# Seven products instead of eight in the second matmul of an MLP: Strassen's scheme on two token tiles of an RWKV-6 + MLP kernel

## Chip, cores and metric

One core of one Trainium2 chip. The metric is the device time of one execution in microseconds (us); 11 runs of the kernel before are known, and one profiled execution. Engines: PE (matmuls; PEld its weight loads), DVE, ACT and POOL (elementwise), SP (issues DMAs). Each works through its own instructions in order and waits on semaphores for the others.

## What is computed

All arrays are float32; B = 4, H = 8 heads, S = 768 steps, D = 48 (so 384 = H·D per token).

```python
state = 0
for t in range(S):                        # RWKV-6, per batch and head
    cur = einsum('bhd,bhe->bhde', u*k[t], v[t])
    y[t] = einsum('bhd,bhde->bhe', r[t], state + cur)
    state = w[t][..., None]*state + einsum('bhd,bhe->bhde', k[t], v[t])
x = y as (B, S, 384)
xn = (x - mean) / sqrt(var + 1e-6) * g_ln
out = x + relu(xn @ w_ch1) @ w_ch2        # w_ch1: 384 x 1536, w_ch2: 1536 x 384
```

## The kernel before, in words

**Work units.** A round is one batch and half of the sequence: 384 tokens, in three tiles of 128. There are eight rounds (0 to 7). A round has two units of four heads each; unit q belongs to round q // 2.

**Recurrence.** For a unit, r and k lie turned, channels on partitions and time along the free axis (`rkT`), and the decays w likewise. Six levels (0 to 5) build the in-chunk attention matrix: at each level `quads` (96 small PE matmuls into `a_ps` for the two units of a round) computes blocks, `grow` (DVE, one 128x768 op for each unit) multiplies r and k by decays for the next level, and `keep` (DVE, a predicated copy) moves the blocks out of PSUM. So quads of a level need the grow of the level before. After level 5 come `ends` (four PE transposes of k into `kn_ps`, each copied by ACT), then `states` (PE `kv`, then a chain of small DVE ops), and `own_outputs`/`outputs` (PE `y`, added up by DVE into `x`).

**Own term.** u·k·r is made from r and k in natural layout (`nat`): `own_products` on DVE in turn 2 and on POOL later, `own_sums` on DVE, `own_term` on POOL. `nat["k"]` and `nat["r"]` have two buffers, by unit parity.

**Loading.** SP issues nearly all DMAs in one queue: `load` (natural layout, three DMAs a tensor), `load_before`, `stage` (runs of w, k, r in four `raw` buffers, shared in turn), the stores. `squares` (DVE 32x32 transposes) turns a staged run into `wT` or `rkT` and so frees its buffer. Rounds 1 and 2 use PE transposes instead.

**MLP.** `moments`/`norm` (DVE, ACT) give `xn`, `turned_x` (PE transposes, ACT) gives `xT`. `mlp` is a generator. It yields after each of 12 steps of the first product (three 128x128x384 matmuls into `h_ps`; ACT's relu writes `h`) and after each of 12 steps of the second (three matmuls into `o_ps`, twelve for a token tile; a DVE add of x, a store). A step is six passes on PE, as a float32 matmul is two passes in the profile. The PSUM tiles `h_ps` and `o_ps` come from one pool, `ps_m`, with two buffers taken in turn; the transposes' PSUM (`ps_t`) also has two.

**Order.** `InOrder` keeps PE, ACT, DVE and POOL (and what goes through `SPO`) in the order in which the program is written; what is issued through `SP` may be placed by the scheduler. The loop `for rnd in range(1, NR + 1)` (called turn 1 to 8 here) does the recurrence of round rnd, level by level, and beside it fills PE with steps of earlier rounds' MLPs. In each of 48 slots (turn, level), `fill(UNTIL[slot], tasks)` spreads the slot's tasks evenly among as many MLP steps as bring the count to `UNTIL`. From slot 17 on, `UNTIL` grows by `MLP_STEPS // NLEV`, 24 // 6 = 4. The MLP of round rnd - 1 joins the list after level 4 of turn rnd (after level 2 in turn 2). The first product so falls into levels 5 to 1, the second into levels 1 to 4 of the next turn. What is left after turn 8, the MLP of round 7, runs by itself.

In the trace of before, turn 2 runs from about 105 to 158 us, turn 3 to 215, and turns 4, 5, 6 and 7 start near 215, 278, 340 and 403 us. Turn 8 starts near 466 us, and the last MLP at 510.7.

## Time and profile before

| | |
|---|---|
| median of 11 runs | 562.02 us (559.16 to 564.7) |
| profiled execution, own time | 562.52 us |
| its span, first to last instruction | 560.8 us |
| mean granted TensorE clock | 0.990 |
| PE busy | 546.8 us (97%) |
| DVE busy | 332.5 us (59%) |
| PE matmuls `h_ps`, 128x384 | 576 passes, 197.2 us |
| PE matmuls `o_ps`, 128x384 | 576 passes, 197.4 us |
| PE small matmuls `a_ps` | 4128, 71.0 us |
| PE's share of the chain that ended last | 81% (DVE 9%, SP queue 4%) |

The profile puts nearly every instruction at line 49 (the helper that records it), so instructions are told apart by the tiles they write and read: `o_ps<-w_sb,h` is the second product, `rkT<-rkT,tot` a grow, `A<-mask,a_ps` a keep, `own_ps<-sel,ruk` an early sum with a moving operand of two columns. A row of a timeline has the start in us, the length, the engine, the operation, out<-in with shapes, and in brackets the idle time ahead of it and what ended it.

### The profile page before, as it was taken

How to read it: one execution, taken by the hardware profiler on the slowest of the kernel's cores; microseconds unless marked ns; L12 is line 12 of the kernel's file. 1: busy time of each engine (PE TensorE's matmuls, PEld its weight loads, DVE VectorE, ACT ScalarE, POOL GpSimd, SP SyncE). 2: the span in 40 equal slices, each digit the busy share in tenths (PEclk: the TensorE clock that was granted, in tenths of full speed). 3: DMA queues.
4: the chain of work that ended last, by engine and by line, in shares of the span. 5: the costliest groups of instructions: out<-in, count | busy, mean ns of one | idle time of the engine just before them, and what ended most of it. 6: DMA issues, size and time to landing. Idle time of an engine off the chain costs nothing.

```text
span 560.8 us, 18190 instructions
## 1 busy us (share of the span) xinstructions
PE 546.8 (97%) x7898; PEld 358.7 (64%) x7898; DVE 332.5 (59%) x654; ACT 169.1 (30%) x363; POOL 135.8 (24%) x157
## 2 busy tenths in 40 slices
PE   9999999998899999999999999999999999999997
PEld 6786665665556666666666666666666666665554
DVE  4889998869688775666585746666563612030000
ACT  3567887502160026201521025201530025202200
POOL 6131010303384029201670039021740000000000
PEclk9889999999989999999999999999999999999999
DMA  9947787155566465646464636444200000000000
GB/s 232 219 104 146 182 222 187 44 115 103 153 150 135 141 130 132 132 114 121 114 125 117 150 94 141 111 128 101 58 1 15 18 15 1 2 29 15 0 15 28
DMA packets 141552, 56.64 MB, mean 101 GB/s; under 512 B 124448, under 2 KB 130720, under 8 KB 141472
## 3 DMA queue, kind: packets, MB, share of 16 engines
q1 hardware_dynamic: 139600, 54.88, 41.7%
q8 instruction: 62, 1.02, 0.7%
q10 hardware_dynamic: 1872, 0.59, 0.4%
q14 instruction: 18, 0.15, 0.1%
HBM read 48.66 MB, written 4.72 MB: 95 GB/s over the span
## 4 chain that ended last, share of the span: by engine, by line
PE 81%; DVE 9%; SPq 4%; ACT 2%; DMA 2%; issue 1%; DVEq 0%; ACTq 0%
PE o_ps L49 32%; PE h_ps L49 27%; PE a_ps L49 9%; PE y L49 4%; DVE w_sb L49 3%; DVE rkT L49 3%; SPq L163 2%; PE kv L49 2%; PE idle L49 2%; PE kn_ps L49 2%; PE xT_ps L49 1%; PE w_ps L49 1%; PE own_ps L49 1%; PE k_ps L49 1%; PE r_ps L49 1%
## 5 line engine op out<-in xcount | busy, mean ns | idle before, releaser
L49 PE MATMUL h_ps<-xT,w_sb 128*128 128x384 f32 x576 | 197.2, 492 | 2.8 <-DVE o L49 1.4
L49 PE MATMUL o_ps<-w_sb,h 128*128 128x384 f32 x576 | 197.4, 492 | 0.1
L49 PEld LDWEIGHTS h_ps<-xT,w_sb 128*128 128x128 f32 x576 | 106.1, 191 | 70.7 <-DVE o L49 2.0
L49 PEld LDWEIGHTS o_ps<-w_sb,h 128*128 128x128 f32 x576 | 105.4, 190 | 65.2 <-ACT h L49 1.0
L49 DVE TENSOR_TENSOR rkT<-rkT,tot 128x768 f32<-128x768 f32 (+1 forms) x96 | 78.5, 859 | 28.6 <-issue 16.9
L49 ACT ACTIVATE h<-h_ps 128x384 f32<-128x384 f32 x96 | 46.9, 489 | 143.9 <-PE h_ps L49 143.7
L49 PEld LDWEIGHTS a_ps<-rkT 48*64 48x64 f32 x4128 | 66.0, 137 | 21.9 <-issue 9.8
L49 PE MATMUL a_ps<-rkT 48*64 48x32 f32 x4128 | 71.0, 221 | 1.2 <-DVE rkT L49 1.0
L49 DVE TENSOR_TENSOR o<-o_ps,x 128x384 f32<-128x384 f32 x24 | 13.3, 553 | 95.9 <-PE o_ps L49 95.9
L49 POOL TENSOR_TENSOR vo<-v,own 128x576 f32<-128x576 f32 x16 | 19.5, 1219 | 96.3 <-DVE own L49 54.8
L49 ACT ACTIVATE rstd<-mv,eps 128x3 f32<-128x3 f32 x8 | 2.4, 296 | 130.1 <-DVE mv L49 130.1
L49 DVE SCALAR_TENSOR_TENSOR s<-s,decay,kv 128x48 f32<-128x48 f32 x160 | 29.3, 258 | 18.6 <-PE kv L49 18.6
L49 POOL TENSOR_TENSOR nat_w<-nat_w,nat_r 128x576 f32<-128x576 f32 x10 | 15.1, 1506 | 104.2 <-DMA nat_w<-in_v_dram 68.6
L49 DVE COPY_PREDICATED A<-mask,a_ps 128x768 f32<-128x768 int8 x32 | 38.4, 1200 | 0.0
L49 DVE TENSOR_TENSOR x<-y,vo 128x288 f32<-128x288 f32 x32 | 13.1, 451 | 30.9 <-PE y L49 30.1
L49 ACT ACTIVATE xT<-xT_ps,g_sb 128x384 f32<-128x384 f32 x24 | 13.6, 580 | 48.4 <-PE xT_ps L49 48.4
L49 DVE TENSOR_TENSOR rkT<-rkT,wT 128x768 f32<-128x768 f32 x16 | 24.9, 1592 | 0.9 <-PE a_ps L49 0.8
L49 DVE TENSOR_REDUCE own<-rk 128x12 f32<-128x576 f32 x12 | 8.9, 740 | 22.5 <-POOL rk L49 22.4
L49 DVE TENSOR_SCALAR w_sb<-w_sb 128x384 f32<-128x384 f32 (+1 forms) x48 | 19.5, 407 | 0.8
L49 PE MATMUL kn_ps<-ident,rkT 128*128 128x128 f32 x96 | 14.4, 285 | 4.0 <-DVE rkT L49 3.1
L49 DVE STREAM_TRANSPOSE rkT<-r_runs 128x384 f32<-128x384 f32 x20 | 15.6, 836 | 4.4 <-DMA r_runs<-in_r_dram 4.4
L49 PEld LDWEIGHTS y<-v,A 64*64 64x64 f32 x384 | 12.8, 134 | 7.6 <-issue 4.9
(88 smaller groups left out, 543.8 us busy)
## 6 DMA issues: line engine op xcount, KB each, us to landing
raw<-in_moe_w_ch_dram SPq DMA_DIRECT2D x24, 384.0 KB, 3.9
w_runs<-in_w_dram SPq DMA_DIRECT2D x79, 70.0 KB, 2.0
k_runs<-in_k_dram SPq DMA_DIRECT2D x79, 70.0 KB, 1.9
r_runs<-in_r_dram SPq DMA_DIRECT2D x79, 70.0 KB, 1.9
v<-in_v_dram SPq DMA_DIRECT2D x48, 96.0 KB, 2.8
out_dram<-o SPq DMA_DIRECT2D x24, 192.0 KB, 2.2
nat_r<-in_r_dram SPq DMA_DIRECT2D x42, 96.0 KB, 3.4
nat_k<-in_k_dram SPq DMA_DIRECT2D x42, 96.0 KB, 3.2
```

Source lines behind the costliest of these rows:

```text
L49: return lambda *args, **kw: self.tc.keep_in_program_order(f(*args, **kw))
L163: eng.dma_start(out=t[ds(HP * j + SQ * e, SQ), 0:n], in_=bass.AP(tensor=src.tensor, offset=first + SQ * e, ap=[[NS * D, SQ], [1, n]]),)
```

## The change

**Second product.** For rounds 2 to 7, `seven` takes the place of the twelve steps. Token tile 2 (Z) stays a plain product, in four steps of three 384-column matmuls. Token tiles 0 and 1 with the halves of the inner dimension (even and odd blocks f, called e) and of the output columns (n) form 2x2 blocks, and seven products of six 128x128x192 matmuls each take the place of eight. They go into the PSUM tiles X and Y (from `ps_m`, with Z the third) and V (from `ps_t`). Steps in order: Z, Z, X, V, V, Z, Z, X (with S2), Y, X (with S3), Y: 11 instead of 12.

**Sums.** DVE makes four sums of 128x768 of the hidden activations for each round (S3, the even block of which V's first product is made, S2, and a last one in place for Y), and adds the products to x in place: seven adds of 192 columns and two of 384, instead of three of 384. `passed()` writes queued sums and adds behind the product of the step in which they come up; the adds of Z, X and Y follow one another near the end, and `y_ps` takes the PSUM buffer of `z_ps`.

**Weight sums.** `weight_sums` computes differences of blocks of `w_ch2` once, on DVE, in slots 17, 18 and 19 (turn 3 level 5, turn 4 levels 0 and 1); one of them in place in `w2_sb`. Their room is a new tile `more` and the second buffers of `nat["k"]` and `nat["r"]`. Units from 8 on therefore use the first buffers alone, and the second unit's k and r are loaded later in the turn (level 4), after POOL is done with the first unit's.

**Turn 2.** r-u-k products and sums: the first unit's at level 2 as before, the second unit's at level 3; its load of k and r for the next round moves with it. DVE transposes of unit 6's r go from level 4 to level 5, where those of unit 7's k and r are too.

**Memory and count.** `hs` is one tile in place of twelve, `low` is a tile in place of a pool, `xn` lies in `kn` buffers (round 0: in a used `rkT`), and `o` is gone. `MLP_STEPS` is 23, and `UNTIL` grows by 23/6.

On DVE the built program has, in turns 4 to 6, this order between the quads of levels 3 and 5: grow, grow, keep (level 3); statistics and norm; three transposes; two adds of V; a transpose; the in-place sum over hs; grow, grow, keep (level 4); the adds of Z, X, Y, X, Y. PE's order there: quads of level 3, V's second step, Z's last two steps, quads of level 4, two groups of `xT` transposes, X with S2, a third group, Y, X with S3, Y, quads of level 5.

```diff
+    def natural(nm, q):
+        return nat[nm][q % 2 if q < 4 * U else 0]
...
-        groups = ((0, 1), (2,)) if rnd == 0 else ((0,), (1,), (2,))
...
-                o = p2.tile([P, H, D], F32, tag="o", name=f"o{name}_{i}")
-                DVE.tensor_tensor(out=o, in0=ps[i], in1=x[:, i], op=ALU.add)
...
+        if rnd > 1:
+            yield from seven(rnd, x, store)
+            return
...
+    def weight_sums(c):
+        if c == 1:
+            DVE.tensor_tensor(out=B_[:, 0, 1], in0=B_[:, 0, 1], in1=B_[:, 0, 0], op=ALU.subtract)
+            return
+        for at, t in pieces(c):
+            n = ds(at, t.shape[1])
+            DVE.tensor_tensor(
+                out=t, in0=more[:, n] if c == 4 else B_[:, 1, 1, n],
+                in1=B_[:, 1, 0, n] if c == 4 else B_[:, 0, 1, n], op=ALU.subtract,
+            )
...
+        Z = tile_of("z_ps")
+        both = [lambda m, e=e: w2_sb[:, 2 * m + e, :] for e in range(2)]
+        product(Z, A(2, 0), both[0], True, range(M // 2))
+        yield
+        sums(S3, A_[:, 0, 0], A_[:, 0, 1], ALU.subtract)
+        product(Z, A(2, 0), both[0], False, range(M // 2, M))
+        yield
+        add(2, 1, Z[:, 0:HD])
+        sums(A_[:, 0, 1], A_[:, 0, 1], A_[:, 1, 1], ALU.add)
+        X = tile_of("x_ps")[:, 0:HD]
+        product(X, A(0, 0), B(0, 0), True)
+        yield
+        add(0, 0, X)
+        sums(S2, A_[:, 0, 1], A_[:, 0, 0], ALU.subtract)
+        V = ps_t.tile([P, RN], F32, tag="t", name=f"v_ps{rnd}")
+        product(V[:, 0:HD], A(0, 1), B(1, 0), True)
+        yield
+        product(V[:, HD:], A(1, 1), lambda m: T(4, m), False)
+        yield
+        add(0, 0, V[:, 0:HD])
+        add(1, 0, V[:, HD:], ALU.subtract)
+        product(Z, A(2, 1), both[1], False, range(M // 2))
+        yield
+        sums(A_[:, 1, 0], A_[:, 1, 0], S2, ALU.subtract)
+        product(Z, A(2, 1), both[1], False, range(M // 2, M))
+        yield
+        due.append(lambda: DVE.tensor_tensor(out=x[:, 2], in0=Z, in1=x[:, 2], op=ALU.add))
+        due.append(lambda: store(2))
+        product(X, lambda m: S2[:, m], lambda m: T(2, m), False)
+        add(0, 1, X)
+        passed()
+        yield
+        Y = tile_of("y_ps")[:, 0:HD]
+        product(Y, A(1, 0), B(0, 1), True)
+        add(1, 1, Y)
+        passed()
+        yield
+        product(X, lambda m: S3[:, m], lambda m: T(3, m), False)
+        yield
+        add(1, None, X)
+        product(Y, A(0, 1), B(1, 1), False)
+        add(0, 1, Y)
+        passed()
+        store(0)
+        store(1)
+        yield
+
+    MLP_STEPS = FC + TT * (FC // KC) - 1
...
-        UNTIL.append(UNTIL[-1] + MLP_STEPS // NLEV)
+        UNTIL.append(UNTIL[-1] + MLP_STEPS / NLEV)
...
-            if rnd == 2 and lev == 2:
-                for q in now:
-                    tasks += each(own_products, [q], [DVE]) + each(own_sums, [q])
-                    tasks += each(load, new[q % U :][:1], "kr")
+            if rnd == 2 and lev in (2, 3):
+                tasks += each(own_products, now[lev - 2 :][:1], [DVE])
+                tasks += each(own_sums, now[lev - 2 :][:1])
+                tasks += each(load, new[lev - 2 :][:1], "kr")
...
+            if slot in (17, 18, 19):
+                tasks += each(weight_sums, ((3,), (1,), (2, 4))[slot - 17])
...
-                if m >= 0:
-                    tasks += each(squares, *turns[m], pairs)
-                if m < 2:
-                    tasks += each(stage, *turns[m + 1], pairs)
+                if rnd == 2 and m > 0:
+                    tasks += each(squares, new[:1], "kr"[m - 1], pairs)
+                    tasks += each(stage, new[1:], "kr"[m - 1], pairs)
+                    if m == 2:
+                        tasks += each(squares, new[1:], "kr", pairs)
+                else:
+                    if m >= 0:
+                        tasks += each(squares, *turns[m], pairs)
+                    if m < 2:
+                        tasks += each(stage, *turns[m + 1], pairs)
...
             if rnd > 1 and new and lev == chain:
                 tasks += each(own_products, new[:1], [POOL])
+                if rnd > 2:
+                    tasks += each(load, new[1:], ["kr"])
```

## Prediction

> **What bounds it now.** I read the page first (busy shares, slices), then PE's waits, then timelines of single engines.

> ```profile
> PE 546.8 (97%) x7898; PEld 358.7 (64%) x7898; DVE 332.5 (59%) x654; ACT 169.1 (30%) x363; POOL 135.8 (24%) x157
> ```
> ```profile
> PE kn_ps L49 <- DVE rkT L49: 3.1, 2, 2.7
> PE h_ps L49 <- DVE o L49: 1.4, 1, 1.4
> ```
> PE is the bound. Its waits are few, and the two largest lie in turn 2 of the loop (at 153.4 and 135.4 us); from 171 us on it never waits over 0.5 us. So a matmul taken away gives back its time unless a new wait eats it. The price of one is in PE's timeline of the last stage and of an early one:
> ```profile
> 533.91 23.38 PE L49 MATMUL o_ps<-w_sb,h 128*128 128x384 f32 x72
> ```
> ```profile
> 20.31 1.50 PE L49 MATMUL own_ps<-sel,ruk 128*128 128x2 f32 x12 [0.24 <-ACT wT L49]
> ```
> A logical product is two passes. 72 passes start within 23.38 us less the last one's 0.16 of pipeline: 322.5 ns each. The own_ps passes stream only 2 columns and still follow at some 112 ns (1.50 less 0.27 over 11): that is the pace of loading 128x128 weights.

> DVE matters too, because Strassen's sums go to it. Its timeline in turn 5 from the level-3 quads on, then PE's in the same stretch:
> ```profile
> 312.11 1.83 DVE L49 TENSOR_TENSOR rkT<-rkT,tot 128x768 f32<-128x768 f32 x2 [2.22 <-issue]
> 313.85 0.96 DVE L49 COPY_PREDICATED A<-mask,a_ps 128x768 f32<-128x768 int8 x1
> 314.72 1.47 DVE L49 BATCH_NORM_STATS2 stats<-x 128x6 f32<-128x384 f32 x3
> ...
> 318.16 1.53 DVE L49 STREAM_TRANSPOSE rkT<-k_runs 128x384 f32<-128x384 f32 x2
> 319.55 1.52 DVE L49 STREAM_TRANSPOSE rkT<-r_runs 128x384 f32<-128x384 f32 x2
> 320.92 0.53 DVE L49 TENSOR_TENSOR o<-o_ps,x 128x384 f32<-128x384 f32 x1
> 321.38 1.80 DVE L49 TENSOR_TENSOR rkT<-rkT,tot 128x768 f32<-128x768 f32 x2
> 323.10 1.00 DVE L49 COPY_PREDICATED A<-mask,a_ps 128x768 f32<-128x768 int8 x1
> ```
> ```profile
> 312.62 6.07 PE L49 MATMUL o_ps<-w_sb,h 128*128 128x384 f32 x18
> 318.62 1.60 PE L49 MATMUL a_ps<-rkT 48*64 48x32 f32 x96
> 320.15 0.55 PE L49 MATMUL xT_ps<-ident,xn 128*128 128x128 f32 x3
> 320.53 2.10 PE L49 MATMUL o_ps<-w_sb,h 128*128 128x384 f32 x6
> ```
> DVE works here without a break from 312.1 to 324.1. Nothing on PE needs its end before the quads at 329.0, so it has 5 us to spare. The change spends them.

> **PE work removed.** Of each MLP from round 2 on (six), 48 passes of 384 columns become 84 of 192. A pass of 192 is in no row: by proportion 161.3 ns; the recorded length of a weight load, 190, is the upper end. I take 162.5, by the 384 row it is nearest to: the load's pace of 112 lies below it. 48 x 322.5 = 15.48 us; 84 x 162.5 = 13.65; six times 1.83 = **-10.98**. At 190 ns it would be 504 x 27.5 ns = 13.9 us worse. [...] The sum goes by the row: whatever is fixed in a pass is part of its 322.5.

> **New wait at Y (levels 4 of turns 4 to 6).** Y takes Z's PSUM buffer (two in `ps_m`), so its first pass waits for the add `x[:, 2] += Z`. In DVE's program order that add stands behind grow and keep of level 4. DVE from the first grow of level 3, start to start in turn 5: grow 2 x 0.87, keep 0.87, statistics and norm 3.44, three transposes 2.08, two adds of V 0.56 (192 columns, from the 0.37 of 288 and 0.46 of 384), transpose 0.69, the sum over hs 0.87 (768 elements, as a grow), grow 2 x 0.86, keep 0.9, the Z add 0.55: 13.42. 312.11 + 13.42 = 325.53. PE: V's second half 1.95 and Z's second half 3.87 take the place of the 18 passes, quads end as before at 320.15, two groups of xT 0.71, X 1.95, the third xT 0.35: ready at 323.2. It waits 2.35 us (0.4 of it at the second xT, which needs V's PSUM buffer back). Turns 4 and 6 show the same rows within 0.3. 3 x 2.35 = **+7.05**. Behind Y stand X, Y's second product, the level-5 quads and all the rest of PE; nothing gives it back, since DVE then waits for PE. Turn 7 has no transposes (2.8 us less): **+0.35**. Turn 8 and the last MLP have no grows: 0. Bounds for one wait: 1.3 (if sums and adds share more of their start) to 3.5 (POOL doubled a keep to 1.88 us elsewhere).

> **Fewer steps, other order.** 23 steps in place of 24 leave seven h steps, not eight, between the level-5 quads and the level-1 quads. DVE's grow of level 0 ends 18.9 us after the level-5 quads, hanging on POOL; PE needs it at 19.6, so it still holds (0.7 to spare). But kn transposes now come three in a row, and the third needs the first one's PSUM copied (ACT 0.47, behind the relu): 0.45 at four turn ends, **+1.8** (0 to 2).

> **Weight sums, turn 4.** 4,608 elements at 959 ns for 768 are 5.8 us of DVE, once. The first 1.4 lie in DVE's wait for POOL (5.6 us idle after 209.0); the next 1.4 stand behind grow of level 0, where all but 0.4 is idle time; the last 2.9 stand in front of the w transposes, which so start 3.3 us later, at 232.9 where it was 229.6. The k and r runs take over their buffers: SP issues them in 8.2 us from the first free buffer (16 at about 0.47, with one long one), the last ends near 242.0 and lands 1.9 later (the median of the issues' view), where DVE wants it at 241.5, since PE arrives 1.5 us earlier. Behind that transpose in DVE's queue are S3, the first Z add and the sum that V's first product needs: 243.9 + 0.7 + 0.9 + 0.3 + 0.9 = 246.7. PE would be there at 244.9. Without the long issue 0.9 is left of these 1.8; I take **+1.4** (0 to 2.5).

> **Turn 2.** Here DVE and SP are late:
> ```profile
> 148.56 0.86 DVE L49 STREAM_TRANSPOSE rkT<-r_runs 128x384 f32<-128x384 f32 x1 [2.27 <-DMA r_runs<-in_r_dram]
> 150.25 0.85 DVE L49 STREAM_TRANSPOSE rkT<-r_runs 128x384 f32<-128x384 f32 x1 [0.83 <-DMA r_runs<-in_r_dram]
> ```
> Unit 5's r-u-k products (2.36 us) go behind the last o add, which ends the 1.4 us wait of h_ps; unit 6's r transposes go behind grow of level 5, which ends the 2.7. PE then runs some 6 us ahead, up to the level-1 quads of turn 3. Those need grow of level 0, and before it in DVE's queue stands unit 7's r transpose. SP now issues six nat loads after unit 5's product (135.6 to 138.8) and six more before r_runs7 (0.55 us each), so this run's last issue ends near 158.0 (156.1 before), landing 1.9 later. Transpose, sums, states and two grows after it: 168.0, where before it was 170.0: -2.0. PE then stands over 3 us, and the rows show what follows such a wait (last columns: PEclk, DMA share, GB/s):
> ```profile
> 150.70:153.40 2.70, 0.01 (x1) 0.00 (x0) 2.66 (x6) 0.49 (x1) 1.50 (x2) 1.00 0.56 159
> 153.40:157.40 4.00, 3.61 (x12) 2.46 (x13) 4.00 (x3) 1.43 (x3) 3.92 (x3) 0.57 0.54 149
> ```
> A low clock after the wait: the matmuls lost about 0.8 us by it. In before that was paid here, after the change it is paid a turn later, perhaps for longer; I charge 0.4 net: **-1.6** (-4 to +1).

> **End.** The last add is 192 wide (-0.2), a second store is issued behind the first (0.33): **+0.15**. Edits at nothing: hs, low and xn in other memory (same order of use), outputs added in place, k and r of one unit loaded later. In turn 5 that load waits on SP for POOL's last use (325.0); behind it in the queue stand two stores and `load_before`, whose own releases come later still. It lands near 330 and POOL takes it at 336.8 at the earliest; were that cover gone, up to 3.4 us a turn.

> **Sum.** -10.98 + 7.05 + 0.35 + 1.8 + 1.4 - 1.6 + 0.15 = -1.8. The profiled execution took 562.52 us (span 560.8, with 1.7 around it), 0.5 above the median of the 11 runs, 562.02: it would take 560.7, the median **560.2**. Its own range, from the bounds that don't move together: 557 to 563.5.

> **Rivals.** (a) The cover at Y holds, because DVE gets through its queue 2.4 us sooner than these rows add up: no 7.4 us of waits, 552.8. For it: DVE is only 59% busy. Against: the stretch above has no gap to give. (b) Slower: the Y waits trip the clock. At Y 1.95 us pass in one piece; 1.4 did not drop the clock at 135.4, 2.7 did at 153.4. A drop costs half of 3.4 us, three times 1.7 = 5.1: 565.3. It decides from a wait of somewhere between those two. [...] (c) Loads do not hide under 192 columns and a pass takes 190 ns: 574.1. Against: the 112 of own_ps.

> **Chances.** Forecast 0.62 (0.36 below -0.3%, 0.21 within, 0.05 above; 0.3% or 1.7 us is about what can be measured here), (a) 0.18, (b) 0.15 (0.03 within, 0.12 slower), (c) 0.05. Faster 0.54, same 0.24, slower 0.22. The range 552.5 to 565.5 leaves out (c), half of (a) and the end of (b).

> **What would show it.** Right: 192-column passes 160 to 165 ns apart; PE idle about 2 us before `y_ps` in turns 4, 5, 6, ended by DVE, and hardly in 7; turns 4 to 6 no shorter than the 62.6 us of before, turn 8 and the last MLP each 1.8 shorter; waits at 135 and 153 gone, one of 2 to 5 us at the first quads of turn 3. Wrong: no wait at `y_ps`, half clock after it, or passes at 190.

## The result and the profile after

The changed kernel takes 570.24 us (median of 12 runs, 567.37 to 572.88); the kernel before, run beside it, 563.09 (47 runs). The ratio is 1.0134, 95% interval 1.0113 to 1.0155: slower by some 7.5 us, where 560.2 was forecast. The profiled execution took 567.69 us (span 566.0), so the median holds about 2.5 us more than the trace shows.

The busy shares and the shares of the chain that ended last, from the page of after:

```profile
PE 541.4 (96%) x8114; PEld 388.4 (69%) x8114; DVE 372.1 (66%) x720; ACT 169.8 (30%) x363; POOL 140.1 (25%) x157
```
```profile
PE 59%; DVE 21%; DMA 5%; SPq 5%; ACT 4%; issue 4%; POOL 1%; DVEq 0%; ACTq 0%; POOLq 0%
```

PE is busy 5.4 us less than before, and yet the span is 5.2 us longer. DVE's share of the last chain went from 9% to 21%: PE now waits for it. Its waits by tile say where:

```profile
PE a_ps L49 <- DVE rkT L49: 5.5, 3, 4.6
PE y_ps L49 <- DVE x L49: 4.5, 4, 2.1
PE kn_ps L49 <- ACT kn L49: 2.7, 8, 0.6
PE xT_ps L49 <- DVE x L49: 2.2, 2, 2.0
```

Columns: total us, times, longest. In before, kn_ps (3.1) and h_ps (1.4) stood at the top, both in turn 2. That of h_ps is gone and that of kn_ps is down to 0.5. In their place one wait of 4.6 stands before quads, and y_ps, xT_ps and the third kn group wait once a turn. (In the text below a wait is counted from start to start of passes less the nominal pass, so it is 0.1 to 0.2 longer than in these lists.)

**Turn by turn.** Turn 2 is entered 0.45 us ahead of before, and turn 3's first outputs end 2.9 us behind it. Turns 4, 5 and 6 take 65.9, 64.0 and 64.3 us where they took 62.6; turn 7 takes 62.1 for 63.1.

**Turn 2, in DVE's and SP's queues.** DVE's timeline of after, then the SP queue's:

```profile
153.74 1.54 DVE L49 STREAM_TRANSPOSE rkT<-r_runs 128x384 f32<-128x384 f32 x2
155.13 1.51 DVE L49 STREAM_TRANSPOSE rkT<-k_runs 128x384 f32<-128x384 f32 x2
159.15 0.86 DVE L49 STREAM_TRANSPOSE rkT<-r_runs 128x384 f32<-128x384 f32 x1 [2.50 <-DMA r_runs<-in_r_dram]
161.51 0.87 DVE L49 STREAM_TRANSPOSE rkT<-r_runs 128x384 f32<-128x384 f32 x1 [1.50 <-DMA r_runs<-in_r_dram]
...
166.08 3.76 DVE L49 TENSOR_TENSOR rkT<-rkT,wT 128x768 f32<-128x768 f32 x2
```
```profile
151.74 1.49 SPq L176 DMA_DIRECT2D nat_w<-in_k_dram  x3
153.33 2.21 SPq L176 DMA_DIRECT2D nat_w<-in_v_dram  x3
155.64 3.70 SPq L165 DMA_DIRECT2D r_runs<-in_r_dram  x8
```

The r runs of unit 7 are issued from 155.64 to 159.34. Two things end just ahead of that: the loads of `nat_w` (155.54), and unit 6's r transposes (155.28), which free the staging buffers. Unit 7's last r transpose ends at 162.4, and the chain behind it (sums, states, grow of level 0) at 169.85. The kernel before came to the same grow at 169.97. So DVE gained nothing, while PE, freed of its two waits, came to the quads 5 us earlier and stood. The same place on PE, and the stage by windows (us, busy us of PE, PEld, DVE, ACT, POOL with counts, then PEclk, DMA share, GB/s):

```profile
167.85 1.51 PE L49 MATMUL a_ps<-rkT 48*64 48x32 f32 x48 [4.57 <-DVE rkT L49]
169.90 1.51 PE L49 MATMUL a_ps<-rkT 48*64 48x32 f32 x48 [0.54 <-DVE rkT L49]
```
```profile
162.54:165.95 3.41, 0.75 (x48) 0.62 (x44) 3.38 (x15) 0.04 (x1) 2.76 (x3) 1.00 0.55 155
...
167.85:171.31 3.46, 2.92 (x96) 2.75 (x96) 3.35 (x8) 0.00 (x0) 3.23 (x4) 0.50 0.67 129
171.31:176.19 4.88, 4.88 (x12) 2.73 (x9) 4.88 (x12) 0.86 (x2) 3.36 (x5) 0.50 0.20 38
```

PEclk is 0.50 from 165.95 to 176.19, 10.24 us. The second quads take 1.51 us, 0.6 longer than at full clock, and the o passes behind them follow at 640 ns where 322.5 is normal: 3.0 us lost beside the wait.

**Turn 5, the wait at Y.** Timelines of DVE and of PE in after:

```profile
327.44 1.81 DVE L49 TENSOR_TENSOR rkT<-rkT,tot 128x768 f32<-128x768 f32 x2
329.16 1.00 DVE L49 COPY_PREDICATED A<-mask,a_ps 128x768 f32<-128x768 int8 x1
330.04 0.55 DVE L49 TENSOR_TENSOR x<-z_ps,x 128x384 f32<-128x384 f32 x1
```
```profile
330.65 2.22 PE L49 MATMUL y_ps<-w_sb,hs 128*128 128x192 f32 x12 [1.79 <-DVE x L49]
```

As forecast: Z's add stands behind grow and keep of level 4, and `y_ps` waits for it.

### The profile page after: what moved, and what is told of

It reads as the page before. It is cut to its first block, busy times and chain, and to the rows that moved or that the text cites. A ratio compares the mean times of both kernels' runs of the same rounds, so it can differ in the third digit from the quotient of the medians.

```text
span 566.0 us, 18702 instructions
## 1 busy us (share of the span) xinstructions
PE 541.4 (96%) x8114; PEld 388.4 (69%) x8114; DVE 372.1 (66%) x720; ACT 169.8 (30%) x363; POOL 140.1 (25%) x157
## 4 chain that ended last, share of the span: by engine, by line
PE 59%; DVE 21%; DMA 5%; SPq 5%; ACT 4%; issue 4%; POOL 1%; DVEq 0%; ACTq 0%; POOLq 0%
PE h_ps L49 21%; DVE rkT L49 9%; PE a_ps L49 6%; PE z_ps L49 6%; PE x_ps L49 4%; PE y_ps L49 4%; PE o_ps L49 4%; PE y L49 4%; SPq L165 3%; PE v_ps L49 3%; DVE A L49 3%; DVE w_sb L49 3%; PE kv L49 1%; DVE s L49 1%; DVE x L49 1%
## 5 line engine op out<-in xcount | busy, mean ns | idle before, releaser
L49 PE MATMUL h_ps<-xT,w_sb 128*128 128x384 f32 x576 | 198.4, 493 | 1.4 <-ACT hs L49 0.7
L49 PEld LDWEIGHTS h_ps<-xT,w_sb 128*128 128x128 f32 x576 | 104.9, 190 | 69.8 <-ACT hs L49 4.8
L49 ACT ACTIVATE hs<-h_ps 128x384 f32<-128x384 f32 x96 | 46.9, 489 | 162.0 <-PE h_ps L49 161.3
L49 DVE TENSOR_TENSOR rkT<-rkT,tot 128x768 f32<-128x768 f32 (+1 forms) x96 | 80.2, 878 | 20.5 <-PE a_ps L49 11.1
L49 PEld LDWEIGHTS a_ps<-rkT 48*64 48x64 f32 x4128 | 66.1, 137 | 23.5 <-issue 11.4
L49 PE MATMUL a_ps<-rkT 48*64 48x32 f32 x4128 | 71.1, 222 | 5.8 <-DVE rkT L49 5.5
L49 PE MATMUL o_ps<-w_sb,hs 128*128 128x384 f32 x144 | 52.7, 513 | 0.1
L49 PE MATMUL z_ps<-w_sb,hs 128*128 128x384 f32 x144 | 48.8, 489 | 0.0
L49 POOL TENSOR_TENSOR vo<-v,own 128x576 f32<-128x576 f32 x16 | 19.4, 1217 | 106.1 <-DVE own L49 72.0
L49 POOL TENSOR_TENSOR nat_w<-nat_w,nat_r 128x576 f32<-128x576 f32 x10 | 16.4, 1641 | 98.6 <-DMA nat_w<-in_v_dram 97.1
L49 DVE SCALAR_TENSOR_TENSOR s<-s,decay,kv 128x48 f32<-128x48 f32 x160 | 29.3, 258 | 14.9 <-PE kv L49 14.9
L49 PEld LDWEIGHTS o_ps<-w_sb,hs 128*128 128x128 f32 x144 | 27.2, 198 | 17.3 <-issue 2.1
L49 DVE COPY_PREDICATED A<-mask,a_ps 128x768 f32<-128x768 int8 x32 | 38.4, 1200 | 0.0
L49 PEld LDWEIGHTS z_ps<-w_sb,hs 128*128 128x128 f32 x144 | 26.9, 190 | 16.6
L49 ACT ACTIVATE rstd<-mv,eps 128x3 f32<-128x3 f32 x8 | 2.4, 296 | 116.8 <-DVE mv L49 116.8
L49 DVE TENSOR_TENSOR x<-y,vo 128x288 f32<-128x288 f32 x32 | 13.1, 450 | 33.1 <-PE y L49 33.1
L49 PE MATMUL y_ps<-w_sb,hs 128*128 128x192 f32 x144 | 25.8, 329 | 4.5 <-DVE x L49 4.5
L49 ACT ACTIVATE xT<-xT_ps,g_sb 128x384 f32<-128x384 f32 x24 | 13.6, 580 | 45.7 <-PE xT_ps L49 45.6
L49 PEld LDWEIGHTS y_ps<-w_sb,hs 128*128 128x128 f32 x144 | 23.4, 190 | 5.4 <-DVE x L49 5.4
L49 DVE TENSOR_TENSOR low<-hs 128x768 f32<-128x768 f32 x12 | 11.6, 964 | 21.5 <-ACT hs L49 21.5
L49 DVE TENSOR_TENSOR rkT<-rkT,wT 128x768 f32<-128x768 f32 x16 | 24.9, 1590 | 0.9 <-PE a_ps L49 0.8
L49 DVE TENSOR_REDUCE own<-rk 128x12 f32<-128x576 f32 x12 | 8.9, 741 | 21.0 <-POOL rk L49 20.9
```

The costliest lines, as they stand in the source:

```text
L49: return lambda *args, **kw: self.tc.keep_in_program_order(f(*args, **kw))
```

## Experiments

Each group of four kernels ran on one chip with its own runs of the kernel before (medians 563.19, 562.54 and 561.45 us), so the ratios with their intervals are compared; 0.1% is 0.56 us.

**1 and 2. The two parts of the change, each alone.** `s_only` keeps Strassen and gives turn 2 its old order; `plain` keeps the new turn 2, the memory and the loads, with plain second products.

```diff
 # s_only
-            if rnd == 2 and lev in (2, 3):
-                tasks += each(own_products, now[lev - 2 :][:1], [DVE])
...
+            if rnd == 2 and lev == 2:
+                for q in now:
+                    tasks += each(own_products, [q], [DVE]) + each(own_sums, [q])
+                    tasks += each(load, new[q % U :][:1], "kr")
...
-                if rnd == 2 and m > 0:
+                if False:
 # plain
-        if rnd > 1:
-            yield from seven(rnd, x, store)
-            return
...
-    MLP_STEPS = FC + TT * (FC // KC) - 1
+    MLP_STEPS = FC + TT * (FC // KC)
...
-            if slot in (17, 18, 19):
-                tasks += each(weight_sums, ((3,), (1,), (2, 4))[slot - 17])
```

> Strassen's scheme, the weight sums and the new memory layout stay; the order of turn 2 goes back to the one of before (both r-u-k products at level 2, transposes of unit 6 and 7 as before). Theory A (turn 2 is the step that failed: the r transposes of unit 6, put behind grow of level 5, free the staging buffers of unit 7 late, so the level-1 quads of turn 3 still start at 170 us, PE stands 4.8 us before them and the clock then halves for 10 us): the level-1 quads start at 170 again, the waits at 135 (1.5) and 153 (2.9) are back, no half clock in turn 3, and the time is about 3.3 us below the changed kernel's 570.2: 567. Rival (Strassen's waits in turns 4 to 7 are the whole loss and turn 2 costs nothing or helps): 570 or above.

> The order of turn 2 and the memory layout of the changed kernel, with the second products of every MLP as plain ones (24 steps, no weight sums). Theory A (turn 2 loses about 3.3 us): 566 to 566.5, with the wait of 4 to 5 us before the level-1 quads of turn 3 and the half clock behind it, and turns 4 to 7 at 62.6 us each as before. Rival (turn 2 is neutral, Strassen's waits are the loss): 563.

Measured: s_only 565.06 us, 1.0045 (1.0014 to 1.0075); plain 565.85, 1.0068 (1.0041 to 1.0096). The waits are where theory A had them. In s_only, 1.53 at 134.6 and 2.85 at 152.6 are back and the quads of turn 3 lose no clock; in plain, the quads wait 3.55 and 0.82 and 6.8 us of half clock lie around them; from turn 4 on its turns take as long as those of before (62.57 us for turns 4 to 6), so the new memory and the later loads cost nothing there. Both parts cost, and the costs add up to 1.13%, at the edge of the changed kernel's interval. s_only gains more than its expectation had, and is still 2 us or so above before. Its profile has 1.94, 1.95, 2.85 and 0.34 us at `y_ps` in turns 4 to 7, and after the third of them the clock halves: nine passes follow at 320 ns where 163 is normal.

**3. Z's add early (`z_early`).**

```diff
         product(Z, A(2, 1), both[1], False, range(M // 2, M))
+        DVE.tensor_tensor(out=x[:, 2], in0=Z, in1=x[:, 2], op=ALU.add)
+        store(2)
         yield
-        due.append(lambda: DVE.tensor_tensor(out=x[:, 2], in0=Z, in1=x[:, 2], op=ALU.add))
-        due.append(lambda: store(2))
```

> The changed kernel with one DVE instruction in another place: the add of Z to x[:, 2], and its store, right behind Z's last product, so ahead of grow and keep of level 4 in DVE's queue. Theory (Y's wait is that of DVE's program order): the waits before y_ps in turns 4 to 7 (0.53, 1.96, 2.30, 0.36 us) fall to at most 0.4 each, 4 us less, and 1 to 2.5 us more where those waits had halved the clock: 563.5 to 566. Rival (DVE's backlog only moves the wait to X's third product or to the level-5 quads): 569 to 570.5.

Measured: 563.52 us, 1.0008 (0.9977 to 1.0039). One DVE instruction in another place, with the store behind it, is worth 1.26% or 7 us, and the kernel is level with before. The same stretch of turn 5, DVE and PE:

```profile
327.67 0.53 DVE L49 TENSOR_TENSOR x<-z_ps,x 128x384 f32<-128x384 f32 x1
328.13 1.78 DVE L49 TENSOR_TENSOR rkT<-rkT,tot 128x768 f32<-128x768 f32 x2
```
```profile
328.91 2.12 PE L49 MATMUL y_ps<-w_sb,hs 128*128 128x192 f32 x12
```

`y_ps` waits no longer; X's third product waits 0.28 in its place. The grow is 0.7 later, which costs nothing, since the quads of level 5 begin 5 us after it. Turns 4 to 7 are together 5.2 us shorter in this trace than in that of after, about what after's four waits at `y_ps` add up to (0.53, 1.96, 2.30 and 0.36). The rest of the 7 us is not placed by a trace. That the clock gave it is not shown: the median granted clock of the runs is 0.9815 in after and 0.982 in z_early.

**4. Idle products in the gap (`warm3`).**

```diff
+            if rnd == 3 and lev == 1:
+                warm(18, "t")
             for q in now:
                 if slot and (lev or rnd < FIRST):
                     quads(q, lev)
```

> The changed kernel with six idle products of 384 columns (12 passes, 3.9 us of PE work that nothing reads) in PE's queue ahead of the level-1 quads of turn 3, where PE otherwise stands for 4.8 us. The wait itself stays. Theory (the standing PE makes the clock halve, and the half clock costs 3.0 us beside the wait): clock at full speed from 163 to 181, the o passes there 322.5 ns apart, 567.2. Rival (the half clock has another cause, or the quads start later for it): 570 or more.

Measured: 571.25 us (6 runs), 1.015 (1.0107 to 1.0193): no gain. In its profile the half clock around the quads is 3.41 us long in place of 10.24, and five o passes pay for it in place of eight. But waits of 1.66 and 1.44 stayed at the two groups of quads (in that run the `nat_w` loads, ahead of the r runs, took 4.8 us of SP for 3.7), and the clock then halved all the same. So it fits that the standing causes the drop; its price in the median isn't shown by this run.

**5 and 6. Both repairs (`s_z`), and V's adds early too (`s_z_v`).** s_z is the diff of s_only with that of z_early. s_z_v adds:

```diff
         product(V[:, HD:], A(1, 1), lambda m: T(4, m), False)
+        add(0, 0, V[:, 0:HD])
+        add(1, 0, V[:, HD:], ALU.subtract)
+        passed()
         yield
-        add(0, 0, V[:, 0:HD])
-        add(1, 0, V[:, HD:], ALU.subtract)
```

> Both edits at once: turn 2 in the order of before (as s_only) and the add of Z early (as z_early). Theory (two separate causes: late r transposes in turn 2, DVE's program order at Y): the savings of 5.2 and 6.7 us add up, 570.2 - 11.9 = 558.3, faster than both kernels. Rival (they share a cause, one of them random drops of the clock that come somewhere anyway): not under 562.

> As s_z, and the two adds of V are put right behind V's second product, ahead of the three transposes in DVE's queue. Theory (the second group of xT waits for V's PSUM buffer, which those adds free): the waits before xT_ps in turns 4 to 6 (1.6 to 2.2, 0.35, 0.28 us) go, 2.2 us less than s_z, and the half clock that followed the one of turn 4 does not come back: 556. Rival (xT waits for DVE's norm, or the next wait takes its place at Y): as s_z.

Measured: s_z 559.85 us, 0.9956 (0.9929 to 0.9983); s_z_v 559.42, 0.9954 (0.9924 to 0.9984). The two causes are separate: from 1.0134 the repairs take 0.89 and 1.26, and together 1.78, the sum within the intervals. With them the scheme is worth its while: 0.44% under before. s_z_v gains nothing over s_z. The xT waits of turns 5 and 6 are gone, but X's third product waits 0.66 and 0.60 there instead of 0.28, and in turn 4 xT waits 1.53 for `xn`, the norm itself, and its second group 0.9 more. (Its trace is of the longest of the 12 runs, 564.37.)

**7 and 8. The two halves of turn 2's change (`z_i`, `z_ii`).** Both have Z's add early. z_i has only the later r-u-k products, z_ii only the later transposes.

```diff
 # z_i
-                if rnd == 2 and m > 0:
+                if False:
 # z_ii
-            if rnd == 2 and lev in (2, 3):
-                tasks += each(own_products, now[lev - 2 :][:1], [DVE])
...
+            if rnd == 2 and lev == 2:
+                for q in now:
+                    tasks += each(own_products, [q], [DVE]) + each(own_sums, [q])
```

> As z_early, but of turn 2's change only one half is kept: unit 5's r-u-k products a level later; the transposes of unit 6 and 7 stay where before had them. Theory (the second half, transposes behind grow of level 5, is what holds unit 7's staging buffers): the wait at 135 is gone, the kn transposes wait 3 to 4.5 us near 152 in its place, the level-1 quads of turn 3 wait under 1.5 us, and the time is at that of s_z, 558 to 560. Rival (the later loads of k and r behind unit 5's product hold SP): quads at 170 after a wait of over 3 us, and about z_early's 563.5.

> As z_early, with only the other half of turn 2's change: r-u-k products of both units at level 2 as before, the transposes of unit 6's r and unit 7 behind grow of level 5. Theory: h_ps waits 1.5 at 135, the kn transposes under 1.5 near 150, the level-1 quads stand 3 us and begin the second half at 170, half clock after it: 562.5 to 564. Rival (the first half is the cause): as s_z, 558 to 560.

Measured: z_i 559.10 us, 0.9951 (0.9925 to 0.9977); z_ii 564.54, 1.0025 (0.9998 to 1.0051). PE's timeline at the place of the wait, of z_i and of z_ii:

```profile
152.82 1.04 PE L49 MATMUL kn_ps<-ident,rkT 128*128 128x128 f32 x6 [3.69 <-DVE rkT L49]
```
```profile
171.21 1.08 PE L49 MATMUL a_ps<-rkT 48*64 48x32 f32 x32 [5.38 <-DVE rkT L49]
```

The later transposes are the cause: 0.7% or 3.9 us against s_z. The later products cost nothing and bring nothing, since PE's 1.5 us at 135 turn up in the wait near 152. How the later transposes hold unit 7's r runs can be read from SP's queue. In the five traces with the later transposes (after, plain, z_early, warm3, z_ii) the `nat_w` loads are issued ahead of these runs, in the nine others behind them, and the runs follow the loads within 0.1 us. The staging buffers were free 0.3 us before the loads ended in after, 1.2 in z_early, 1.4 in warm3, 2.6 in z_ii, and 0.4 us after them in plain. So in four of the five it is the loads in front that the runs wait for, and the buffers come next. No run has the later transposes with the loads behind.

**9. Weight sums moved up (`s_z_sums`).**

```diff
-            if slot in (17, 18, 19):
-                tasks += each(weight_sums, ((3,), (1,), (2, 4))[slot - 17])
+            if slot in (16, 17):
+                tasks += each(weight_sums, ((3,), (1, 2, 4))[slot - 16])
```

> As s_z, with the weight sums moved up: the first (1.4 us of DVE) into level 4 of turn 3, the other two (4.3 us) into level 5 of turn 3, where DVE waits for POOL. Theory (in turn 4 xT waits for a DVE that is late by those sums): the wait of 1.6 to 2.2 us before xT_ps at about 258 us falls to the 0.35 of turns 5 and 6, 1.3 us less, and 0.7 more where that wait had halved the clock: 558 to 558.5. Rival (the sums now delay turn 3's grow of level 5, or grow of level 0 and so the level-1 quads of turn 4): a wait of over 1 us near 208 or 225 in its place, as s_z.

Measured: 561.31 us, 0.9993 (0.9971 to 1.0015), so 2 us above s_z: the rival. xT in turn 4 waits 0.34 instead of 1.72, but the level-1 quads of turn 4 now wait 1.10 and 1.35 for grow of level 0, with 3.41 us of half clock behind them. The 5.8 us of sums find no free place there.

**10. The short slot (`s_z_kn`).**

```diff
-        n = int(until + 0.01) - done
+        n = int(until + 0.34) - done
```

> As s_z, with the 23 steps rounded so that the turn's short slot is level 1 and not level 5: an h step stands again between the second and the third group of kn transposes. Theory (the third group waits for the first one's PSUM copy): the 0.46 us before kn_ps at four turn ends go, 1.8 us less: 558. Rival (the step taken from level 1 brings the waits of xT and X nearer, by the 2 us that PE arrives earlier there): as s_z or above.

Measured: 557.60 us (9 runs), 0.9920 (0.9893 to 0.9947): 0.36% or 2.0 us below s_z, as the theory had it. The 0.46 at four turn ends are gone. But its trace is of the longest of the nine runs (558.97) and has some 3.4 us more wait than that of s_z at xT and X in turns 4 to 6, as the rival said. So the gain is measured, and that it comes from the kn waits alone is not shown.

**11. SP's queue (`z_i_7`).** z_i with `load` of unit 7's k and r behind the staging of unit 6's runs.

```diff
-                tasks += each(load, new[lev - 2 :][:1], "kr")
+                if lev == 2:
+                    tasks += each(load, new[:1], "kr")
...
+            if rnd == 2 and lev == 3:
+                tasks += each(load, new[1:], "kr")
```

> As z_i, with one more move on SP: the six loads of k and r of unit 7 (3.1 us of issue) behind the sixteen issues of unit 6's runs, no longer ahead of them. Theory (SP's queue, never idle from 129 to 163 us, sets when unit 6's r lands, and the kn transposes wait for it): the 3.9 us before kn_ps near 152 fall to about 1, the half clock behind it goes, the level-1 quads of turn 3 begin near 168: 2 to 4 us less than z_i, 555 to 557. Rival (POOL's products, which need those loads, or unit 7's runs are then late): the level-1 quads wait over 2 us, as z_i.

Measured: 558.78 us, 0.9944 (0.9919 to 0.9969), against 0.9951 of z_i: no difference to be told, and the 2 to 4 us of the theory did not come. In the built program only the three loads of r moved; those of k stayed ahead. The wait before kn_ps fell to 1.47 in the profile, but the clock halved after it all the same (from 155.40 three h passes take 2.12 us, where three at full clock take 1.13), and the level-1 quads came no earlier after the start of the turn than in z_i.

**12. All of it (`all`).** z_i_7 with the diffs of s_z_sums, s_z_kn and s_z_v.

> z_i_7 with the weight sums moved up, the steps rounded as in s_z_kn and V's adds early as in s_z_v. If the parts are separate causes: 559.1 less 3 (SP), 1.5 (sums), 1.8 (kn) is 553 to 554, 1.6% below the kernel before. Rival (DVE's backlog in turns 4 to 6 turns each into a wait somewhere else): 556 to 558.

Measured: 556.09 us (6 runs), 0.9907 (0.9874 to 0.9939). It beats both kernels, by 0.9% and by some 2.2%. It is the rival's number: X's third product waits 0.66, 1.90 and 1.37 in turns 4 to 6, and turn 4's level-1 quads 1.35.

## Why the prediction was wrong

**PE work: right.** 192-column passes start by turns 162 and 163 ns apart, 162.6 in the mean (162.5 assumed). Six times 48 x 322.5 less 84 x 162.6 is -10.9, for -10.98. Twice 162.6 is only 2.7 ns over 322.5, so next to nothing in a pass is fixed; rival (c) is out.

**Wait at Y: right.** 2.35 a turn with xT's share: 0.35 + 1.96 in turn 5, 0.27 + 2.30 in turn 6, 0.36 in turn 7 (0.35). z_early shows that the cause named, DVE's program order, was the true one. One bound had no ground: the keep of 1.88 us that the prediction laid to POOL is that of level 1. It takes 1.86 to 1.88 in all eight rounds of before, in five of them with POOL idle, while two keeps of levels 3 and 4 with POOL busy throughout took 0.98 and 1.01.

**kn order: right.** 0.46 at four turn ends, and in s_z_kn they are gone.

**Weight sums: right in kind, wrong in place.** V's first product does not read the in-place sum (what the text on the change says there is wrong): in after it runs at 248.1, the sum at 250.6. That sum is read by S2 and by Y's first product. DVE's lateness came up 14 us later instead, at turn 4's second xT (2.20, where turn 5 has 0.35), and the clock halved for 3.41 us behind it:

```profile
261.99 0.90 PE L49 MATMUL xT_ps<-ident,xn 128*128 128x128 f32 x3 [2.04 <-DVE x L49]
```

So in turn 4 hardly any wait was left for Y (0.53), and the two come to 2.73 us where 2.35 + 1.4 was forecast. That the weight sums were behind it fits s_z_sums, where that xT waits 0.34, but PE came some 4 us later to that turn there, so it isn't shown.

**Turn 2: the step that failed, -1.6 forecast.** plain gives +3.8 us for it alone, the difference of after and s_only +5.0. The wait before turn 3's first quads was foreseen (2 to 5 us; 4.6 in the list); what failed is that DVE's chain would end 2.0 us earlier than before. SP's last issue was put at 158.0 and the end of the grow at 168.0; they came at 159.3 and 169.85. The `nat_w` loads in front were in the forecast, but the six `nat` loads of unit 7 began 0.5 us later than forecast, and those of `nat_w` took 0.63 us each instead of 0.55. That the r runs' buffers were not free before 155.28 was left out; without the loads in front the runs could have started only 0.3 us earlier. z_i and z_ii show that the later transposes, which moved these runs from 151.8 (z_i) to 155.6 (after), were the wrong move. And the clock, charged with 0.4 net, cost 3.0. Of the 9.3 us between -1.8 and +7.5, turn 2 makes 5.4 by plain and 6.6 by s_only.

**The clock: a rival that should have been in the sum.** The terms without turn 2 add up to -0.2; s_only came out at 1.0045, +2.5, and its profile has a half clock at Y that the sum did not have. Rival (b) had the mechanism and the price of one drop (half of 3.4 us, as in before, where the clock is at 0.50 from 153.88 to 157.29; the passes behind s_only's wait at Y in turn 6 lost 1.7), and at 0.15 it was put too low. There is no such bound on the wait as it looked for "between those two" (1.4 and 2.7): 1.66 and 1.44 us at warm3's quads were followed by a half clock (0.50 from 175.35 to 178.76), 2.30 at Y in after and 2.90 in s_z_kn were not (1.00 in the step behind). Waits of about 2 us come four or five to a run, and each has its own chance. By the granted clock, 0.9815 in the median of after's runs and 0.990 in that of the 29 of before that ran beside s_only, after has some 10 us more at half clock. At the 3.0 us that 10.24 cost in turn 3 (an estimate for the rest) that is about 3 of the 7.5 us.

## What to carry to other kernels

When an engine that set the pace is relieved, follow the next consumer's chain, not the engine: here PE's two waits went and the grow it then needed ended at the same 169.9. For a step that is moved later, ask which buffer its reading frees, which DMA waits for that buffer, and which loads come to stand ahead of that DMA in the queue. And look at what stands ahead of a short instruction that another engine waits for: the add of Z, moved by three places in DVE's queue, gave back 7 of the 7.5 us.

## What was not expected of the hardware

```profile
387.91:391.32 3.41, 1.27 (x8) 1.28 (x9) 2.35 (x4) 0.07 (x1) 0.00 (x0) 1.00 0.13 40
391.32:394.73 3.41, 3.41 (x12) 3.41 (x11) 0.36 (x1) 0.00 (x0) 0.00 (x0) 0.50 0.87 171
```
```profile
391.23:394.64 3.41, 1.55 (x11) 1.29 (x9) 3.41 (x5) 0.58 (x1) 0.00 (x0) 1.00 0.00 0
394.64:398.05 3.41, 3.13 (x19) 3.14 (x20) 0.84 (x3) 0.00 (x0) 0.00 (x0) 1.00 0.55 126
```
```profile
147.16:150.57 3.41, 1.48 (x5) 0.57 (x3) 2.41 (x5) 0.49 (x1) 0.88 (x1) 1.00 0.56 155
150.57:153.98 3.41, 1.95 (x12) 1.48 (x13) 3.41 (x4) 1.34 (x3) 3.16 (x4) 1.00 0.56 156
153.98:157.40 3.42, 3.42 (x14) 1.92 (x12) 3.42 (x4) 1.98 (x6) 3.33 (x3) 1.00 0.75 157
```
```profile
150.47:153.88 3.41, 0.70 (x5) 0.46 (x5) 3.37 (x6) 0.49 (x1) 1.98 (x2) 1.00 0.54 155
153.88:157.29 3.41, 3.04 (x10) 2.00 (x9) 3.41 (x3) 1.43 (x3) 3.33 (x3) 0.50 0.56 152
```

PE busy for 1.27 us of a step: half clock in the next. 1.55: none. The wait of 2.90 fell across two steps (1.48 and 1.95) and cost no clock, where before's 2.87 lay in one (0.70) and did. The other steps of before and after that lie behind 40 us, ran at full clock, held only matmuls on the whole array (128*128 in the rows) and were busy for less than 2.6 us go the same way: 0.64 in before (556.65) and 0.78 in after (561.90) were followed by a half clock, 2.05 in before (133.40) and 2.58, 2.48 and 2.56 in after (148.89, 326.38, 329.79) by none. warm3 has one at 1.29 (332.36) with a half clock behind it. Between 1.29 and 1.48 none of these steps lies, so where it turns is not shown. Of the steps behind 40 us that ran at half clock themselves, those of 3.04 in before (153.88), 2.95 (261.53) and 3.41 in after (172.78) were followed by full clock, and in turn 3 of after those of 1.51 (165.95, 48 quads) and 2.88 (169.37, 48 of 51 passes quads) by half clock again.

With the small matmuls in the step (quads, 48*64) busy time alone does not tell. After's step of 2.44 at 43.07, with 16 quads among 46 passes, was followed by no half clock; its step of 1.85 at 258.11, with 96 quads, was, as was warm3's of 2.17 at 171.94, with 81 passes, most of them quads, and this one of s_z_v at 2.97, with 176 quads and no wait over 0.5 us:

```profile
121.04:124.45 3.41, 2.97 (x177) 2.74 (x170) 2.85 (x3) 0.00 (x0) 0.00 (x0) 1.00 0.86 168
124.45:127.87 3.42, 3.42 (x6) 1.91 (x7) 3.02 (x10) 0.30 (x1) 0.00 (x0) 0.50 0.54 107
```

The step at the same place is 2.97 in before (119.75) and 2.98 in after (118.17), with 147 and 163 quads, and no drop behind it. What the quads count for is open.

So whether a wait of 2 to 3 us cost clock in these windows went by how it lay on the grid, and the grid lies differently in each trace: counted from the start of the span, its steps begin 0.28 us past a multiple of 3.413 in before, 2.11 in after and 1.26 in warm3. Only one run of each kernel has a trace, but the granted clock is known for every run, and the times follow it: of s_only's runs (562.8 to 568.5, for the same program) the five at 0.994 or more took 562.8 to 563.5 us, and the four at 0.985 or less 567.8 to 568.5.
